# One branch a step for the second products of a mixture-of-experts layer, and later requests for the rows of the norms

## The chip, the cores and the metric

The kernel runs on one core of one Trainium2 chip. The metric is the device time of one execution in microseconds (us); smaller is better. Times of runs are medians of several executions; a profile is one execution more, taken with the hardware profiler on.

## What is computed

Three layers in a row, all in fp32, over 2304 tokens of width 512. The matrix products split each fp32 number into a high and a low part and take three products (high by high, high by low, low by high).

```python
x = windowed_attention(q, k, v)                 # window 64, 4 x 576 tokens, 8 heads
xn = x / sqrt(mean(x * x) + 1e-6) * rms_g       # first MoE, dense, d_ff 1536
x = (silu(xn @ w_gate) * (xn @ w_val)) @ w_out
e = argmax(x @ wg2); p = softmax(x @ wg2)[e]    # second MoE, 8 experts, d_ff 1024
out = p * (relu(x @ w1[e]) @ w2[e])             # each token through its own expert
```

## The kernel before

The order of every engine's instructions is the order in which the program is written out (a manual schedule); nothing is reordered later. TensorE (PE) is fed by one helper, `mm` at L57, so all matrix products have that line. LDWEIGHTS, branches and other instructions of PE's sequencer stand in the profile as PEld and PEldq.

**The first MoE.** The 2304 tokens are six sub-blocks of 384 (`subs`), in four blocks of two, two, one and one (`BLOCKS`). The loop over `units` (L900 on) goes block by block through 12 slices of d_ff, and one unit is one slice for one sub-block: 24 products of 384 columns (gate and value), SiLU on ScalarE (ACT, L649), a product on VectorE (DVE, L650), a split into `hh` and `hl` (L651, L652), and then the nine output products of the unit before. Beside that, generators hand out further work piece by piece: `beside` (L274) resumes each task while the unit has budget; a task that yields "step" gets a rest of 99, so it is not resumed again in this unit.

- `conversion` / `w_conv` (L391): the weights of the first block come as 64-bit words, half a slice (768 KB) at a time into three buffers `st`, by a DMA that SyncE (SP) issues at L389, and are turned into fp32 by ACT (L472, L464, L465) and DVE (L429, L434, L438). The ACT part of the next half stands on ACT ahead of the next unit's SiLU.
- `norms` / `norm(i)` (L308, L312): the norms of sub-blocks 2 to 5, one after the other. Each asks for its rows (L323, on SP, into the one buffer `xr`), yields, squares them on ACT (L332), sums, takes a root by Newton steps, and writes the split `xt` (L368, L371). The last thing that reads `xr` is the DVE subtraction at L371. The next norm's request is written out in the same piece that ends the norm before, and SP waits at it until `xr` is free.
- L923: in every second unit from 2 to 16, SP issues a fill of 1 MB for one expert (`xs<-x2dram`).

SP's queue is in order: an instruction that waits holds all that are behind it.

**The second MoE.** `route` has sorted the tokens by expert into `xs` and `table`. `items` (L809) are the pieces of work: two of two tiles for expert 0 (a tile is 128 tokens), then one "full" item of up to four tiles for each of experts 1 to 7. Each item has 8 steps `(i, f)`, one for each 128 of d_ff, 72 in all (`steps2`). Step k (L1100 on) does the first products of k (`first_mm`, 12 of n columns, into bank k % 2), the second products of step k - 1 (`out_c`, three for each tile j, summed over f into bank 4 + j), then `relu(k)` on ACT and DVE (L1020, L1021), the split of the weights for step k + 2 (`c_split`, L552 and L554) and loads of weights (L822). Transposes of the next item's tokens stand behind steps 2 to 5 (`c_transpose`, L856). At f = 0 `c_out` scales and writes out the item before (L1050 on ACT for tiles 0 and 2, L1048 on DVE for 1 and 3, L1051 on POOL), which empties banks 4 to 7.

How many of an item's tokens are real is known only at run time. `count[e]` is loaded into a register of PE, and `cases(i, body, unit)` (L984) writes the body out once for each possible size and branches to the right one by halving: for a full item in units of 64 the sizes 512, 448, 384, 320, 256, with three comparisons on the way to 256, which is the last in the code; in units of 128 the sizes 512, 384, 256. A body has its `first_mm` at that size (never under 256 columns) and its `out_c` for as many tiles. With three matrix products to a tile, a full item's step with f > 1 is written out as 5 x 12 first products and 12 + 12 + 9 + 9 + 6 second ones: 108 pairs of LDWEIGHTS and MATMUL, of which 18 to 24 run. The order of bodies in the code is 512, 448, 384, 320, 256.

Step f = 1 has two sets of branches, one around the first and one around the second products; step f = 0 has one around the first products and one around the second products of the item before. `last_tiles` (L1030) finishes the last item.

Of the kernel before, what the change touches and what calls it, by code (L numbers as in the profile page):

```python
# [26 lines left out]
P = 128  # L27
# [23 lines left out]
def attention_moe_moe_kernel(ctx, tc, qT, kT, vw, w1p, rms_g, wg2, wg2T, w2p, out):  # L51
# [4 lines left out]
    def mm(o, l, r, start, stop):  # L56
        nc.tensor.matmul(o, l, r, start=start, stop=stop)  # L57
# [54 lines left out]
    def xt_views(at, n):  # L112

        return [xt_t[:, a:a + 4 * n].rearrange("p (c t) -> p c t", c=4) for a in (at, at + 4 * n)]

    def big(which):
        return xr_p.tile([P, 4, 512], F32, name="xr" if which == 0 else "sq")
# [156 lines left out]
    def beside(tasks, budget):  # L274

        for t in tasks:
            t.rest = 0.0
        while budget > 0:
            can = [t for t in tasks if not t.done and t.rest <= 0 and t.want != "bank"
                   and not (callable(t.want) and not t.want())]  # L280
            if not can:
                break
            cost = can[0].piece()
            budget -= cost
            for o in tasks:
                if o is not can[0]:
                    o.rest -= cost
        return budget

    def on_bank(tasks, bk):  # L290

        for t in tasks:
            if t.want == "bank" and not t.done:
                return t.piece(bk)
        return 0.0
# [16 lines left out]
    def norm(i):  # L312
        t0, nt, _ = subs[i]
        if i == 1:

            xr, sq = (t[:, :4 * SUB].rearrange("p (c t) -> p c t", c=4) for t in wraw_t[:-3:-1])
        else:
            xr, sq = big(0), big(1)
        done = 0
        while done < nt:  # L320
            b, s = divmod(t0 + done, S)
            step = min(nt - done, S - s)
            nc.sync.dma_start(xr[:, :, done:done + step],  # L323
                              xdram[b][:, :, s:s + step].rearrange("h p t -> p h t"))
            done += step
        for _ in range(4 if i < 2 else 1):
            yield "step"
        for c in range(4):
            if i < 2:
                nc.gpsimd.tensor_tensor(out=sq[:, c, :nt], in0=xr[:, c, :nt], in1=xr[:, c, :nt], op=ALU.mult)  # L330
            else:
                nc.scalar.activation(sq[:, c, :nt], xr[:, c, :nt], AF.Square, scale=1.0)  # L332
            if i < 2 and c % 2:
                yield "step"
        yield "step"
        for a, b in ((0, 1), (2, 3), (0, 2)):
            (nc.gpsimd if i < 2 else nc.vector).tensor_add(sq[:, a, :nt], sq[:, a, :nt], sq[:, b, :nt])
            if i == 0:
                yield "step"
            elif i > 1:  # L340
                yield 0.5
        if i == 1:
            yield "step"
        bk = yield "bank"
        mm(bk[:, :nt], ones, sq[:, 0, :nt], True, True)
        m, y, t = (sq[:, k, :nt] for k in (1, 2, 3))
        nc.vector.tensor_scalar(out=m, in0=bk[:, :nt], scalar1=1.0 / DM, scalar2=1e-6, op0=ALU.mult, op1=ALU.add)
        yield 0.5
        nc.vector.tensor_scalar(out=y.bitcast(I32), in0=m.bitcast(I32), scalar1=-0.5, scalar2=1597463007.0,
                                op0=ALU.mult, op1=ALU.add)  # L350
        yield 0.4
        sc = 1.0
        for _ in range(NEWTON):

            nc.scalar.activation(t, y, AF.Square, scale=1.0 / sc)
            yield "rest"
            nc.vector.tensor_mul(t, t, m)
            yield 0.6
            nc.vector.scalar_tensor_tensor(out=y, in0=t, scalar=-3.0, in1=y, op0=ALU.add, op1=ALU.mult)
            yield 0.6  # L360
            sc = sc * -2.0
        yield lambda: i < NXT or free[0] >= i - NXT + 1
        xh_t[i], xl_t[i] = xh, xl = xt_views(i % NXT * 8 * SUB, nt)
        for c in range(5):
            if c < 4:
                nc.vector.scalar_tensor_tensor(out=xr[:, c, :nt], in0=xr[:, c, :nt], scalar=gs_sb[:, c:c + 1],
                                               in1=y, op0=ALU.mult, op1=ALU.mult)
                nc.scalar.copy(xh[:, c], xr[:, c, :nt])  # L368
                yield 0.5
            if c > 0:  # L370
                (nc.gpsimd if i == 0 else nc.vector).tensor_tensor(  # L371
                    out=xl[:, c - 1], in0=xr[:, c - 1, :nt], in1=xh[:, c - 1].bitcast(F32), op=ALU.subtract)
                yield 0.0 if i == 0 else 0.5
        normed[0] = i
# [153 lines left out]
    def split_mm(o, lh, ll, rh, rl, start, stop):  # L528
        mm(o, lh, rh, start, False)
        mm(o, lh, rl, False, False)  # L530
        mm(o, ll, rh, False, stop)
# [123 lines left out]
    def last_mm(w, h, banks, f0, f1):  # L655

        wh, wl, hh, hl = wh_t[w, "o"], wl_t[w, "o"], hh_t[h], hl_t[h]
        for j, bk in banks:
            ts = slice(j * P, (j + 1) * P)
            split_mm(bk, hh[:, ts], hl[:, ts], wh, wl, f0, f1)  # L660
# [9 lines left out]
    def out_b(u):  # L670
        k, i = units[u]
        last_mm(k, ("b", u), enumerate(out_banks(i)), u == starts[i], u == stops[i])
# [147 lines left out]
    def c_load(w):  # L820
        if w < E * NF2:
            nc.sync.dma_start(wring[w % NRING], w2p[w // NF2, w % NF2])  # L822
# [77 lines left out]
    for u, (k, i) in enumerate(units):  # L900
        n = steps[k][0]
# [82 lines left out]
    def cases(i, body, unit=P // 2):  # L984

        e, t0, T = items[i]

        def between(lo, hi):
            if lo == hi:
                return body(lo * unit)  # L990
            mid = (lo + hi) // 2
            with tc.If(count[e] > t0 * P + mid * unit) as more:
                between(mid + 1, hi)
            with more.Else():
                between(lo, mid)

        if i == 0:
            body(T * P)
        elif T == 4:
            between(2 * P // unit, T * P // unit)  # L1000
        else:
            unit = P
            between(1, T)

    def first_mm(k, n):
        i, f = steps2[k]
        wh, wl = wh_t[K0 + k, "a"], wl_t[K0 + k, "a"]
        xh, xl, n = xh_t["c", i], xl_t["c", i], max(n, 2 * P)
        for c in range(4):
            w = slice(c * P, (c + 1) * P)  # L1010
            split_mm(bank[k % 2][:, :n], wh[:, w], wl[:, w], xh[:, c, :n], xl[:, c, :n], c == 0, c == 3)
# [12 lines left out]
    def out_c(k, n, j0=0):  # L1024
        f = steps2[k][1]
        last_mm(K0 + k, K0 + k, [(j, bank[4 + j]) for j in range(j0, -(-n // P))], f == 0, f == NF2 - 1)

    NL = len(steps2) - 1
# [71 lines left out]
    for k, (i, f) in enumerate(steps2):  # L1100
        if i == 0:
            first_mm(k, 2 * P)
            if k == 0:
                out_b(len(units) - 1)
            else:
                on_bank([end], bank[3])
                beside([end], 99)
                out_c(k - 1, 2 * P)
        elif f == 1:

            cases(i, lambda n: first_mm(k, n))
            cases(i, lambda n: out_c(k - 1, n), P)
        elif f > 0:
            j0 = 2 if k >= NL - 1 else 0
            cases(i, lambda n: (first_mm(k, n), out_c(k - 1, n, j0)))
        else:
            parts = [lambda: cases(i, lambda n: first_mm(k, n)), lambda: cases(i - 1, lambda n: out_c(k - 1, n), P)]
            for part in parts[::-1] if i == 1 else parts:
                part()
        relu(k)  # L1120
        if k == 0:
            evac(len(units) - 1)
        if f == 0 and i > 0:
            c_split(k + 2, parts="a")
            c_out(i - 1)
            c_split(k + 2, parts="o")
        else:
            c_split(k + 2)
        while i > 0 and later:
            c_load(later.pop(0))  # L1130
        if i == 0:
            if f == NF2 - 1:
                end.finish(bank[3])
                load_count(1)
                for j in range(2):
                    c_transpose(1, j, bank[2 + j % 2])
            continue
        if f == 5:
            load_count(i + 1)
        beside([over], 0.4)  # L1140
        if i == len(items) - 1 and f == 3:

            nc.gpsimd.drain()
        if f in (2, 3, 4, 5):
            c_transpose(i + 1, f - 2, bank[2 + f % 2])
        if f == 6:
            c_gather(i + 2)
# [85 lines left out]
```

## Time and profile before

| | us |
|---|---|
| median of 3 runs | 870.89 (869.74 to 874.89) |
| the profiled execution | 877.16 |
| span of the profiled execution, first to last instruction | 875.3 |
| PE busy with matrix products in it | 842.8 |
| mean granted clock of PE, share of full | 0.989 |

The span is cut by the profile into the attention (to about 130 us), the first MoE (to about 594 us) and the second (to about 870 us). The profiled execution is longer than the median of the runs by 6.27 us. In the views, a time in square brackets is how long the engine sat idle before an instruction and what ended that; "issue" means that nothing which the profile shows ended it. Idle time of an engine matters only where PE waits for it.

### The profile page before, as it was taken

What the parts mean: (1) busy time and instruction counts of PE and PEld (TensorE: products, weight loads), DVE (VectorE), ACT (ScalarE), POOL (GpSimd) and SP (SyncE); (2) the same over time, 40 slices, a digit from 0 to 9 for tenths busy, and PEclk for the clock granted to TensorE, in tenths of its full rate; (3) what the DMA queues carried; (4) which work ended last, traced back from release to release, by engine and by line L of the source; (5) the groups of instructions that cost most, each with busy time, mean ns of one, the idle gap of its engine ahead of it and who ended that gap; (6) DMA issues with size and microseconds to landing.
All of it is one profiled execution on the core that took longest, in us unless ns stands there. A gap on an engine that the chain in (4) does not pass through costs nothing. (4 is left out here: it accounts for less than half of the span.)

```text
span 875.3 us, 13523 instructions
## 1 busy us (share of the span) xinstructions
PE 842.8 (96%) x4667; PEld 775.9 (89%) x4667; DVE 607.8 (69%) x1472; ACT 450.0 (51%) x993; POOL 212.2 (24%) x227
## 2 busy tenths in 40 slices
PE   7999999999899999999999999999999999988997
PEld 7999988999799999999989999988888898867886
DVE  6789878788685566666478864697685765655454
ACT  5787787777573433322243424334564645554353
POOL 3348573444242000000500032004300120121011
PEclk9999999999899999999999999999999999999999
DMA  7988618895922300000220016533674655552000
GB/s 215 303 267 265 201 69 228 194 227 121 248 103 97 108 19 19 1 0 1 73 73 1 1 37 176 199 107 133 213 258 151 208 204 172 182 198 82 12 35 29
DMA packets 47071, 114.49 MB, mean 131 GB/s; under 512 B 10223, under 2 KB 14703, under 8 KB 46834
## 3 DMA queue, kind: packets, MB, share of 16 engines
q1 hardware_dynamic: 42386, 103.50, 38.6%
q0 software_dynamic: 4576, 9.47, 2.9%
q8 instruction: 77, 1.26, 0.6%
q14 instruction: 32, 0.26, 0.1%
HBM read 93.90 MB, written 31.10 MB: 143 GB/s over the span
## 5 line engine op out<-in xcount | busy, mean ns | idle before, releaser
L57 PE MATMUL bank<-xt,wha 128*128 128x384 f32 (+3 forms) x1728 | 422.6, 329 | 14.6 <-issue 9.6
L57 PEld LDWEIGHTS bank<-xt,wha 128*128 128x128 f32 x1728 | 306.1, 190 | 31.1 <-issue 11.0
L57 PE MATMUL bank<-xt,wla 128*128 128x384 f32 (+3 forms) x864 | 281.9, 326 | 0.7 <-DVE wla L554 0.7
L57 PEld LDWEIGHTS bank<-xt,wla 128*128 128x128 f32 x864 | 164.2, 190 | 2.2 <-DVE wla L554 1.7
L57 PE MATMUL bank<-who,hl 128*128 128x512 f32 x382 | 151.6, 397 | 0.6 <-DVE hl L1021 0.6
L57 PE MATMUL bank<-wlo,hh 128*128 128x512 f32 x382 | 151.8, 397 | 0.0
L57 PE MATMUL bank<-who,hh 128*128 128x512 f32 x382 | 151.2, 396 | 0.5 <-ACT hh L651 0.2
L651 ACT CAST hh<-t 128x384 fp32r<-128x384 f32 x72 | 37.0, 513 | 144.5 <-DVE t L650 142.2
L554 DVE TENSOR_TENSOR wla<-wraw,wha 128x512 fp32r<-128x512 f32 (+1 forms) x112 | 97.8, 874 | 8.1 <-ACT wha L552 7.4
L1021 DVE SCALAR_TENSOR_TENSOR hl<-bank,hh 128x512 fp32r<-128x512 f32 (+1 forms) x71 | 44.6, 628 | 80.8 <-ACT hh L1020 79.7
L650 DVE TENSOR_TENSOR t<-t,bank 128x384 f32<-128x384 f32 x72 | 39.8, 552 | 85.1 <-PE bank L57 61.9
L552 ACT CAST wha<-wraw 128x512 fp32r<-128x512 f32 (+1 forms) x113 | 87.1, 771 | 7.6 <-DVE wraw L438 7.0
L1020 ACT ACTIVATE hh<-bank 128x512 fp32r<-128x512 f32 (+1 forms) x71 | 39.1, 550 | 97.8 <-PE bank L57 96.8
L57 PEld LDWEIGHTS bank<-who,hl 128*128 128x128 f32 x382 | 72.4, 190 | 17.6 <-DVE hl L1021 1.4
L1051 POOL DMA_INDIRECT out_dram<-x,ix x32 | 34.9, 1091 | 218.2 <-ACT x L1050 211.2
L57 PEld LDWEIGHTS bank<-who,hh 128*128 128x128 f32 x382 | 72.8, 191 | 12.1 <-issue 0.6
L57 PEld LDWEIGHTS bank<-wlo,hh 128*128 128x128 f32 x382 | 72.7, 190 | 11.1
L57 PE MATMUL bank<-kt,qz 128*128 128x128 f32 x288 | 76.3, 406 | 5.3 <-DMA kt<-in_kT_dram 4.5
L552 ACT CAST who<-wraw 128x512 fp32r<-128x512 f32 x111 | 68.7, 619 | 22.5 <-PE bank L57 20.7
L57 PEld LDWEIGHTS bank<-kt,qz 128*128 128x128 f32 x288 | 72.4, 334 | 5.8 <-issue 4.5
L554 DVE TENSOR_TENSOR wlo<-wraw,who 128x512 fp32r<-128x512 f32 x99 | 68.0, 687 | 13.1 <-ACT who L552 6.0
L715 DVE SCALAR_TENSOR_TENSOR junk<-x,wg_bc 128x512 f32<-128x512 f32 x120 | 75.9, 686 | 0.0
(168 smaller groups left out, 977.3 us busy)
## 6 DMA issues: line engine op xcount, KB each, us to landing
wraw<-in_w2p_dram SPq DMA_DIRECT2D x64, 512.0 KB
st<-in_w1p_dram SPq DMA_DIRECT2D x24, 768.0 KB
wraw<-in_vw_dram SPq DMA_DIRECT2D x16, 512.0 KB
xs<-x2dram SPq DMA_DIRECT2D x8, 1024.0 KB
qz<-in_qT_dram SPq DMA_DIRECT2D x32, 144.0 KB
xdram<-wraw SPq DMA_DIRECT2D x16, 288.0 KB
x2dram<-x SPq DMA_DIRECT2D x18, 256.0 KB
kt<-in_kT_dram SPq DMA_DIRECT2D x15, 288.0 KB
```

The lines of the kernel that those rows point to most:

```text
L57: nc.tensor.matmul(o, l, r, start=start, stop=stop)
L552: nc.scalar.copy(wh, src[:, r])
L554: e.tensor_tensor(out=wl, in0=src[:, r], in1=wh.bitcast(F32), op=ALU.subtract)))
L650: nc.vector.tensor_tensor(out=t, in0=t, in1=v, op=ALU.mult)
L651: nc.scalar.copy(hh[:, :nt], t)
L715: nc.vector.scalar_tensor_tensor(out=junk, in0=x2, scalar=1.0, in1=wg_bc[:, e], op0=ALU.mult, op1=ALU.mult, accum_out=lg[:, j, e:e + 1])
L1020: nc.scalar.activation(hh[:, :n], bank[k % 2][:, :n], AF.Relu, scale=1.0)
L1021: nc.vector.scalar_tensor_tensor(out=hl[:, :n], in0=bank[k % 2][:, :n], scalar=0.0, in1=hh[:, :n].bitcast(F32), op0=ALU.max, op1=ALU.subtract)
L1051: d = nc.gpsimd.indirect_dma_start(out=out[:, :], in_=y, in_offset=None, out_offset=bass.IndirectOffsetOnAxis(ap=ix[:, j, 0:1], axis=0), b ...
```

## The change

Two edits. In `norm`, for sub-blocks 3, 4 and 5, a "step" is yielded before the rows are asked for, so that the request is written out one unit later. In the loop over `steps2`, the branches are cut differently:

- full items, f > 0: one set of branches around `first_mm(k)` and the second products of tiles 2 and 3; the second products of tiles 0 and 1 follow behind the branches, without any. So f = 1 has one set where it had two. For k of 70 and 71 the step is as before.
- full items, f = 0: branches around the first products as before, then tiles 0 and 1 of the item before without a branch, then branches around its tiles 2 and 3 only. For the item behind the two-tile items, as before.
- the second two-tile item (i = 1): no branches around the first products of f = 0 and 1, which always have 256 columns.

```diff
@@ norm @@
         else:
+            if i > 2:
+                yield "step"
             xr, sq = big(0), big(1)
@@ the loop over steps2 @@
-        elif f == 1:
-
+        elif i == 1:
+            if f < 2:
+                if f == 0:
+                    out_c(k - 1, 2 * P)
+                first_mm(k, 2 * P)
+                if f == 1:
+                    cases(i, lambda n: out_c(k - 1, n))
+            else:
+                cases(i, lambda n: (first_mm(k, n), out_c(k - 1, n)))
+        elif f > 0:
+            cases(i, lambda n: (first_mm(k, n), out_c(k - 1, n, 2)))
+            if k < NL - 1:
+                out_c(k - 1, 2 * P)
+        else:
+            j0 = 0 if i == 2 else 2
             cases(i, lambda n: first_mm(k, n))
-            cases(i, lambda n: out_c(k - 1, n), P)
-        elif f > 0:
-            j0 = 2 if k >= NL - 1 else 0
-            cases(i, lambda n: (first_mm(k, n), out_c(k - 1, n, j0)))
-        else:
-            parts = [lambda: cases(i, lambda n: first_mm(k, n)), lambda: cases(i - 1, lambda n: out_c(k - 1, n), P)]
-            for part in parts[::-1] if i == 1 else parts:
-                part()
+            out_c(k - 1, j0 * P)
+            cases(i - 1, lambda n: out_c(k - 1, n, j0), P)
```

Written out, a full item's step with f > 1 becomes 5 x 12 first products, 6 + 6 + 3 + 3 + 0 second ones in the bodies and 6 behind them: 84 pairs. A whole full item goes from 822 pairs (87 + 87 + 6 x 108) to 663 (75 + 7 x 84). The products that run are the same ones.

## Rows read from the trace of the kernel before

**Rows 1.** The page's first lines: span and busy time of each engine.
```profile
span 875.3 us, 13523 instructions
...
PE 842.8 (96%) x4667; PEld 775.9 (89%) x4667; DVE 607.8 (69%) x1472; ACT 450.0 (51%) x993; POOL 212.2 (24%) x227
```
**Rows 2.** PE's timeline in the first MoE: its longest idle time there.
```profile
225.93 1.65 PE L57 MATMUL bank<-sq,ones 128*128 128x384 f32 x2 [4.09 <-DVE t L650]
```
**Rows 3.** ACT's timeline there: when the next half of the weights is used.
```profile
209.43 0.91 ACT L472 ACTIVATE wraw<-st 128x768 f32<-128x768 f32 x1
...
222.36 0.89 ACT L472 ACTIVATE wraw<-st 128x768 f32<-128x768 f32 x1 [5.44 <-DMA st<-in_w1p_dram]
```
**Rows 4.** SP's timeline there: start us, us, what is issued.
```profile
198.22 0.33 SPq L389 DMA_DIRECT2D st<-in_w1p_dram  x1
208.54 0.38 SPq L323 DMA_DIRECT2D xr<-xdram  x1
208.96 0.51 SPq L923 DMA_DIRECT2D xs<-x2dram  x1
209.58 1.24 SPq L389 DMA_DIRECT2D st<-in_w1p_dram  x2
```
**Rows 5.** SP's waits, whole run: us in total, times, longest us.
```profile
SPq L323 <- DVE xt L371: 57.8, 3, 32.1
```
**Rows 6.** A window: length, busy of PE, PEld, DVE, ACT, POOL, clock, DMA share, GB/s.
```profile
202.60:208.80 6.20, 6.20 (x34) 5.83 (x33) 6.02 (x8) 4.39 (x7) 3.69 (x2) 1.00 0.00 0
```
**Rows 7.** The same view of two stretches at the lower clock.
```profile
746.90:750.30 3.40, 3.40 (x14) 2.92 (x13) 1.29 (x2) 1.10 (x2) 0.00 (x0) 0.50 0.75 288
...
224.70:231.50 6.80, 5.58 (x15) 4.97 (x16) 3.77 (x6) 4.39 (x7) 1.01 (x1) 0.50 0.96 178
```
**Rows 8.** PE's first products by shape, 644 to 869.7 us: busy, mean ns | idle before.
```profile
L57 PE MATMUL bank<-xt,wha 128*128 128x256 f32 x256 | 50.2, 294 | 10.8 <-issue 9.6 <-ACT xt L858 1.2
...
L57 PE MATMUL bank<-xt,wha 128*128 128x320 f32 x64 | 14.6, 315 | 0.7 <-ACT who L552 0.3 <-ACT wha L552 0.3
```
**Rows 9.** PE's timeline in the second MoE: the longest idle times.
```profile
690.11 0.50 PE L57 MATMUL bank<-xt,wha 128*128 128x256 f32 x2 [1.17 <-ACT xt L858]
...
746.05 0.50 PE L57 MATMUL bank<-xt,wha 128*128 128x256 f32 x2 [1.91 <-issue]
...
774.62 0.50 PE L57 MATMUL bank<-xt,wha 128*128 128x256 f32 x2 [2.28 <-issue]
780.10 0.50 PE L57 MATMUL bank<-xt,wha 128*128 128x256 f32 x2 [1.95 <-issue]
797.50 0.50 PE L57 MATMUL bank<-xt,wha 128*128 128x256 f32 x2 [3.02 <-issue]
```
**Rows 10.** The branches of `cases` (L992): all, then one (ns min/median/max, first and last).
```profile
L992 PEldq COMPARE_BRANCH  x218: 65/208/5391, 621.0 to 863.5; - x109
...
L992 PEldq COMPARE_BRANCH  x1: 3221/3221/3221, 771.3 to 771.3; - x1
```
**Rows 11.** PE's timeline: two steps of a 256-column item that follow each other.
```profile
763.72 0.40 PE L57 MATMUL bank<-xt,wha 128*128 128x256 f32 x2
...
766.54 0.40 PE L57 MATMUL bank<-xt,wha 128*128 128x256 f32 x2
```
**Rows 12.** The page's DMA queues: packets, MB, share of 16 engines.
```profile
q8 instruction: 77, 1.26, 0.6%
```
**Rows 13.** `last_tiles`, where a body is empty: L992, and PE around it.
```profile
L992 PEldq EVENT_SEMAPHORE  x1: 51/51/51, 865.9 to 865.9; - x1
...
865.44 0.39 PE L57 MATMUL bank<-who,hl 128*128 128x512 f32 x1
865.98 0.47 PE L57 MATMUL bank<-who,hh 128*128 128x512 f32 x1
```
**Rows 14.** Emptying banks 4 and 6 (ACT), then the next second products (PE).
```profile
706.51 1.27 ACT L1050 ACTIVATE x<-bank,ix 128x512 f32<-128x512 f32 x2
...
708.79 0.39 PE L57 MATMUL bank<-who,hh 128*128 128x512 f32 x1
```

## The prediction

> **What bounds it.** I read the page first: PE is busy for 842.8 of 875.3 us [rows 1], so a gain can only come from time in which PE stands still or runs at the lower clock. PE's timeline gives those places, and I followed each to its cause.
>
> In the first MoE there is one large place. [...] The cause stands on ACT: L472 waits 5.44 us for its half of the weights [rows 3], and the SiLU behind it comes late. Why those weights are late is seen on SP: between 198.55 and 208.54 it issues nothing, because it waits at the norm's request L323 for DVE's L371, and the fill and the weight load stand behind it [rows 4, 5]. Meanwhile the DMA engines move nothing at all: share 0.00, 0 GB/s from 202.60 to 208.80 [rows 6].
>
> In the second MoE, PE's idle time by shape says where to look: 10.8 us stand before the first products of 256 columns, 0.7 before those of 320, nothing before 384 and 448 [rows 8]. The 256 products are four full items (256 rows are 4 x 64), the short ones. The five longest gaps are 1.17, 1.91, 2.28, 1.95 and 3.02 us [rows 9]; the rest of the 10.8 is one of about 0.5. Most are marked "issue", so no engine ended them. The branches tell: a branch takes 208 ns in the median and 5391 at most, and the one just before the gap of 2.28 us takes 3221 [rows 10]. The instruction behind it was not there yet: instructions come by DMA, 77 packets of 1.26 MB together, 16.4 KB each [rows 12]. Behind three of the gaps the clock is at half for 3.40 us with PE busy throughout; one of the three stands in [rows 7]. That is 3 x 1.7 = 5.1 us. Gaps and clock together: 10.8 + 0.7 + 5.1 = 16.6 us. These are what the branches cost now.
>
> **The norm's request.** Norm 3's load moves past the fill and one weight load on SP. Their order becomes: weight load (198.22), fill at once, next weight load as soon as its buffer is free, then the request, which still can't go before 208.54. So the rows come no sooner and no later on SP, but behind two transfers, 1 MB and 0.77 MB, that now use the idle stretch. From 198.6, at the 178 and 288 GB/s of the stretches in [rows 7], 1.8 MB take 6 to 10 us, so the weights land by 209. They are wanted one unit after 209.43, at about 215.7: 6 us to spare. ACT's wait of 5.44 us goes, and with it the idle time and the half clock behind it: -6.9 us. What is late next is the norm itself: squares and Newton steps come one unit later, with two dozen units before their result is used, so this costs 0; were that cover gone, it would be one unit's squares on ACT, under 2 us. Bounds: 0 if the next weight load is late instead, -6.9 if nothing is. I take -6.9, since 6.2 us of idle DMA time are there to be used. The requests of norms 4 and 5 account for most of SP's 57.8 us of waiting [rows 5], but hold only stores that PE does not wait for: 0.
>
> **The branches in short items.** A full step's written code falls from 108 pairs to 84, what runs stays. One such step takes 766.54 - 763.72 = 2.82 us [rows 11]. For the same length of code PE now passes through 108 / 84 as much work, 3.63 us instead of 2.82: each wait for code is met by 0.8 us more work. Taking 0.8 from each gap leaves 0.4, 1.1, 1.5, 1.15 and 2.2. The two of 1.91 and 2.28 stand right behind step f = 1, where a second set of branches with 27 written pairs and 6 that run makes the distance between two waits short; that set goes, so I take these two as gone. What stays is 0.4 + 1.15 + 2.2 = 3.7 us, and behind the longest one stretch of low clock, 1.7: 5.4 us. The gain is 16.6 - 5.4 = 11.2 us. Bounds: 16.6 if all goes; 3.2 if the gaps fall only as the written code of an item does (822 to 663, 19%); below nothing in the third rival.
>
> **The empty body.** At f = 0 the branch around tiles 2 and 3 of the item before has an empty body if that item was short. Such a body is seen once, in `last_tiles`: instead of products there is a semaphore instruction of 51 ns that lets PE run dry, and the next product starts 0.54 us after the one before, where 0.23 is usual: 0.31 lost [rows 13]. Three full items come behind a short one. In each, the three branches of f = 1 then find PE with no work queued: 3 x 0.208. So 0.31 + 0.62 = 0.93, three times: +2.8 us. Bounds: 0.9 if the branches are hidden, 10.6 if each also meets a wait of 3.22 as in [rows 10]. I take 2.8, as code was there for most branches (median 208 ns).
>
> [...]
>
> **At no cost.** In items with more than two tiles, tile 2 now comes ahead of tile 0, so at f = 1 bank 6 is wanted first. ACT has emptied it at 706.51 + 1.27 = 707.78, and the second products start at 708.79 [rows 14]: 1.0 us to spare; without that cover it would cost at most that one move, 0.6 us, in three items. The branches dropped from the two-tile item were hidden (no gap there by the branches): 0, at best a few tenths.
>
> **Sum.** -6.9 - 11.2 + 2.8 = -15.3 us against the profiled execution's 877.16: 861.9. The median of the runs is 6.27 us lower. If these runs have every stall that the profile shows, they go to 870.89 - 15.3 = 855.6; if the 6.27 us are stalls that they do not have, they end where the profile ends, at 861.9. Waits for code vary from one execution to the next, and the runs themselves lie 5.1 us apart, so I take the middle: 859.
>
> **Rivals**, each on the same middle (3.1 us under the profile's own sum).
>
> 1. The gaps stay. A wait arises when the path enters new code, not by how far it jumps, and falls only with the amount of code: -6.9 - 3.2 + 2.8 = -7.3, 866.7. For it: two branches waited 4 to 5.4 us, more than any step's work, and nothing makes a load itself faster. Against: the gaps stand only in short items, where much code is passed per us of work.
> [...]
> 2. All gaps go and the empty bodies cost the least: -6.9 - 16.6 + 0.9 = -22.6, 851.4. For it: nothing waits in items of 384 and 448. Against: 5391 ns is more than a step.
> 3. Slower: every shortened body ends as the empty one does. If the sizes under 512 must make up for missing tiles with a semaphore instruction that runs PE dry, 7 items x 7 steps lose 0.31 each, 15.2 us, and the lead that hides waits for code is lost too, so those gaps stay: -6.9 + 15.2 + 2.8 = +11.1, 885. It turns the result from 0.08 us a step on, if the gaps stay. Against it: bodies with fewer tiles exist before, and among 218 branches the trace has one such instruction [rows 10, 13].
> 4. The first MoE's stall comes back with the next weight load, because fill, rows and weights want the DMA engines together: -11.2 + 2.8, 865.6. Against: the idle 6.2 us.
>
> **Chances.** Forecast 0.48, rivals 0.18, 0.22, 0.05, 0.07. The range, 849.5 to 867.5, holds the forecast's bounds and rivals 1, 2 and 4. A change of 1% (8.7 us, below 862.2) is about what the measurement can tell. Faster by more than that: most of the forecast and rival 2, and a quarter of rivals 1 and 4, 0.67; within 1%: 0.28; slower: 0.05.
>
> **What would show it.** Right: no wait of ACT for `st` in the first MoE, SP's fill at about 198.6, no low clock between 200 and 240 us; in the second MoE gaps before the 256 products of about 4 us instead of 10.8, few branches over 3000 ns, and fewer than 77 instruction packets; three semaphore instructions at L992 more, each with about 1 us of idle PE. Wrong: gaps as large as before behind other steps, semaphore instructions in every step, or a stall at the next weight load.

## The result, and the profile after

The changed kernel takes 859.45 us in the median of six runs (858.1 to 864.49), the kernel before 872.0 in six runs on the same chip (869.74 to 874.89): ratio 0.9864, 95% interval 0.9834 to 0.9894. In a second comparison it was 858.58 against 873.23, ratio 0.9831 (0.981 to 0.9852). So it is faster by 1.4 to 1.7%, some 12.5 to 14.7 us. The forecast was 859.0, in a range of 849.5 to 867.5.

The page's first lines, of after:

```profile
span 857.1 us, 13511 instructions
...
PE 834.9 (97%) x4667; PEld 770.3 (90%) x4667; DVE 606.8 (71%) x1472; ACT 449.3 (52%) x993; POOL 210.6 (25%) x227
...
q8 instruction: 68, 1.11, 0.6%
```

The span is shorter by 18.2 us than that in [rows 1]. The same 4667 products take 7.9 us less busy time, since none before the last instructions runs at the lower clock any more (mean granted clock 1.00, 0.989 before), and the idle time fell by 10.3 (875.3 - 842.8 = 32.5 against 857.1 - 834.9 = 22.2). There are 68 packets of instructions where [rows 12] has 77.

**The first MoE.** SP's timeline of after (L391 is the weight load, L925 the fill, L325 the norm's request), and ACT's next use of the weights:

```profile
198.58 0.48 SPq L925 DMA_DIRECT2D xs<-x2dram  x1
204.16 0.33 SPq L391 DMA_DIRECT2D st<-in_w1p_dram  x1
208.53 0.38 SPq L325 DMA_DIRECT2D xr<-xdram  x1
210.45 0.33 SPq L391 DMA_DIRECT2D st<-in_w1p_dram  x1
```
```profile
209.42 0.91 ACT L474 ACTIVATE wraw<-st 128x768 f32<-128x768 f32 x1
215.90 0.92 ACT L474 ACTIVATE wraw<-st 128x768 f32<-128x768 f32 x1
218.40 1.75 ACT L334 ACTIVATE sq<-xr 128x384 f32<-128x384 f32 x4
221.56 0.91 ACT L474 ACTIVATE wraw<-st 128x768 f32<-128x768 f32 x1
```

Against [rows 4] the fill goes out 10.4 us sooner and the weight load 5.4 sooner, while the norm's request stays at 208.5, because its buffer is free no earlier. ACT finds its weights at 215.90 without waiting; in [rows 3] it waited until 222.36. What the DMA engines and PE do there, the same windows as before:

```profile
202.60:208.80 6.20, 6.20 (x34) 5.81 (x33) 6.02 (x8) 4.40 (x7) 3.69 (x2) 1.00 0.99 107
208.80:215.30 6.50, 6.50 (x36) 6.10 (x35) 5.32 (x7) 4.75 (x7) 1.72 (x1) 1.00 1.03 349
...
222.00:232.00 10.00, 10.00 (x56) 9.59 (x55) 8.42 (x10) 7.43 (x11) 5.14 (x3) 1.00 0.82 228
```

The 6.2 us in which nothing was moved [rows 6] have a DMA share of 0.99, and PE is busy throughout at clock 1.00, where [rows 2, 7] had 4.09 us of idle time and half the clock.

**The second MoE.** PE's products by shape from 637 to 851.5 us, idle time behind the bar; compare [rows 8]:

```profile
L57 PE MATMUL bank<-xt,wha 128*128 128x256 f32 x256 | 48.6, 287 | 2.5 <-ACT x L1052 1.2 <-ACT who L554 0.5 <-issue 0.4
L57 PE MATMUL bank<-xt,wla 128*128 128x256 f32 x128 | 36.3, 283 | 1.5 <-issue 1.5
L57 PE MATMUL bank<-xt,wha 128*128 128x448 f32 x64 | 18.6, 372 | 0.6 <-ACT x L1052 0.6
L57 PE MATMUL bank<-xt,wha 128*128 128x384 f32 x64 | 16.8, 342 | 0.6 <-ACT x L1052 0.6
L57 PE MATMUL bank<-xt,wha 128*128 128x320 f32 x64 | 14.6, 315 | 0.2 <-issue 0.2
```

Of 11.5 us of idle time, 5.4 are left. PE's timeline names most of it:

```profile
676.99 0.38 PE L57 MATMUL bank<-xt,wla 128*128 128x256 f32 x1 [1.51 <-issue]
...
699.24 0.61 PE L57 MATMUL bank<-xt,wha 128*128 128x384 f32 x2 [0.58 <-ACT x L1052]
...
759.49 0.50 PE L57 MATMUL bank<-xt,wha 128*128 128x256 f32 x2 [1.20 <-ACT x L1052]
...
769.63 0.50 PE L57 MATMUL bank<-xt,wha 128*128 128x256 f32 x2 [0.53 <-ACT who L554]
779.66 0.51 PE L57 MATMUL bank<-xt,wha 128*128 128x256 f32 x2 [0.44 <-issue]
787.14 0.67 PE L57 MATMUL bank<-xt,wha 128*128 128x448 f32 x2 [0.59 <-ACT x L1052]
```

And the branches, now L994:

```profile
L994 PEldq COMPARE_BRANCH  x200: 70/208/2857, 617.6 to 845.6; - x100
L994 PEldq EVENT_SEMAPHORE  x4: 51/51/51, 698.7 to 847.7; - x4
```

Four semaphore instructions stand where [rows 13] has one. The three new ones belong to the idle times 0.58, 1.20 and 0.59, each in front of step f = 1 of a full item behind a short one: 2.37 us that the change brought with it. What remains of waits for code is 1.51 + 0.53 + 0.44 + 0.15 = 2.6 us, with no low clock behind it (the longest branch now takes 2857 ns, 5391 in [rows 10]). The names in the brackets of the gaps (ACT L1052, L554) are only the last update before the product: L1052 empties the banks of the item before and `who` is a weight of the second products, and a first product reads neither.

### The profile page after: what moved, and what is told of

Read it like the earlier page. It is cut to its first block, busy times and chain, and to the rows that moved or that the text cites. A ratio compares the mean times of both kernels' runs of the same rounds, so it can differ in the third digit from the quotient of the medians.

```text
span 857.1 us, 13511 instructions
## 1 busy us (share of the span) xinstructions
PE 834.9 (97%) x4667; PEld 770.3 (90%) x4667; DVE 606.8 (71%) x1472; ACT 449.3 (52%) x993; POOL 210.6 (25%) x227
## 5 line engine op out<-in xcount | busy, mean ns | idle before, releaser
L554 ACT CAST wha<-wraw 128x512 fp32r<-128x512 f32 (+1 forms) x113 | 87.1, 771 | 8.1 <-DVE wraw L440 7.7
L57 PEld LDWEIGHTS bank<-who,hh 128*128 128x128 f32 x382 | 71.9, 188 | 11.9 <-issue 0.6
L554 ACT CAST who<-wraw 128x512 fp32r<-128x512 f32 x111 | 68.7, 619 | 17.5 <-PE bank L57 16.1
```

Source lines behind the costliest of these rows:

```text
L554: nc.scalar.copy(wh, src[:, r])
```

## The experiments

Two comparisons, each against the kernel before on one chip.

**The changed kernel again.** 

> The changed kernel once more, for comparison with the others of this call on the same chip. Both theories: ratio to the kernel before 0.985 to 0.988, about 859.5 us.

858.58 us, ratio 0.9831 (0.981 to 0.9852), a little lower than expected. Its profile has the same three idle times in front of f = 1 (0.58, 1.19, 0.67), and not the one of 1.51: waits for code differ from one execution to the next.

**The norm's edit alone.**

```diff
         else:
+            if i > 2:
+                yield "step"
             xr, sq = big(0), big(1)
```

> The kernel before with the norm's edit alone. Theory (SP's wait at the request held the weight load, in every execution): ACT's wait of 5.44 us for the weights and PE's idle 4.09 us go, the half clock from 224.7 to 231.5 goes, -6.9 us, ratio about 0.992, and the second half of the run has its gaps as before (12 to 17 us of idle time and half clock in the profile). Rival (the stall is of the profiled execution only, or moves to the next weight load): within 2 us of the kernel before, ratio 0.998 or more.

867.26 us, ratio 0.9937 (0.9915 to 0.996): -6.0 us. The low clock and the idle time of the first MoE are gone, and SP's order there is that of after, to 0.1 us. In the second MoE the idle time stands as before, 11.9 us before the 256 products where [rows 8] has 10.8, with two stretches of low clock instead of three (the views by shape of the experiments cover 636 to 880 us, so their counts differ a little):

```profile
L57 PE MATMUL bank<-xt,wha 128*128 128x256 f32 x257 | 50.2, 293 | 11.9 <-issue 9.2 <-ACT xt L860 2.7
```

The rival's ratio of 0.998 lies outside the interval, so the stall isn't one of the profiled execution alone, and the theory holds.

**Norm 3 alone.**

```diff
+            if i == 3:
+                yield "step"
```

> The kernel before with the norm's edit for sub-block 3 alone; norms 4 and 5 ask as before. Theory: the whole gain of the norm's edit (6.0 us alone) is that of norm 3, ratio 0.992 to 0.995, and SP still waits some 48 us in two waits at L323. Rival: part of it comes from norms 4 and 5, ratio over 0.996.

866.73 us, ratio 0.9929 (0.9908 to 0.9951), -6.1: the whole gain is that of norm 3. SP's remaining waits:

```profile
SPq L325 <- DVE xt L373: 51.8, 3, 32.1
```

In [rows 5] they were 57.8 us. The expectation had two waits of 48 us together, and there are three: norm 3's own request still waits some 4 us until 208.58, 6 us less than before. The waits of norms 4 and 5 are still there and cost nothing that the runs show (-6.1 here, -6.0 with all three moved).

**The branches' edit alone** (the second part of the change's diff).

> The kernel before with the second MoE's edit alone. Theory: the stall of 4.09 us in the first MoE stands as before; the gaps in the second MoE fall to about 5 us with the empty bodies' in it, no low clock there; against the median of the runs this is what is left of the 12.5 us after the norm's 6.9: -5 to -6 us, ratio 0.993 to 0.994. Rival (the gaps of the second MoE are mostly of the profiled execution): -2 us or less, ratio 0.998 or more.

864.94 us, ratio 0.9913 (0.9893 to 0.9933): -8.3 us, more than expected. The idle time of the first MoE stands there, in its old size (the low clock behind it lasts 3.4 us in this profile, 6.8 in that of before):

```profile
226.16 1.65 PE L57 MATMUL bank<-sq,ones 128*128 128x384 f32 x2 [4.28 <-DVE t L650]
```

-6.0 and -8.3 add up to -14.3, and both together gave -14.65 in the same comparison: within the intervals the two edits add up. On the profile's scale this edit gave 877.16 - 865.45 = -11.7 us.

**No empty body.**

```diff
-            j0 = 0 if i == 2 else 2
+            j0 = 0 if i == 2 else 1
             cases(i, lambda n: first_mm(k, n))
             out_c(k - 1, j0 * P)
             cases(i - 1, lambda n: out_c(k - 1, n, j0), P)
```

> The changed kernel, but at f = 0 of the full items from the fourth item on, tile 0 alone stands ahead of the branches and tiles 1 to 3 stand inside, so that no body is empty. Theory (the empty body lets PE run dry and bares the three branches that follow; the profile of after has 0.58 + 1.20 + 0.59 = 2.37 us there): the three semaphore instructions at the line of the branches go, these three gaps go, and the time falls by 2.4 us against the changed kernel, to about 857, ratio to before about 0.983. Rival (PE would stand still there anyway, because the branches of f = 1 follow at once on those of f = 0): the gaps stay at 0.4 us or more each and the time falls by under 1 us.

856.28 us (854.73 to 857.34), ratio 0.9816 (0.9796 to 0.9837), 2.3 us under the changed kernel in the same comparison. The runs of the two overlap a little (the changed kernel's go down to 856.9), but the profile shows where the time went: the three semaphore instructions are gone, and with them the idle time before the products of 384 and 448 columns and most of that before 256.

```profile
L994 PEldq EVENT_SEMAPHORE  x1: 51/51/51, 843.4 to 843.4; - x1
...
L57 PE MATMUL bank<-xt,wha 128*128 128x256 f32 x264 | 49.8, 286 | 0.8 <-ACT xt L860 0.8
...
L57 PE MATMUL bank<-xt,wha 128*128 128x448 f32 x64 | 18.5, 370 | 0.0
L57 PE MATMUL bank<-xt,wha 128*128 128x384 f32 x64 | 16.7, 341 | 0.0
```

The rival falls. This is the fastest version that ran.

**More code that never runs.**

```diff
+        elif T == 4 and unit < P:
+            between(2 * P // unit, T * P // unit + 2)
         elif T == 4:
             between(2 * P // unit, T * P // unit)
...
-                return body(lo * unit)
+                return body(min(lo * unit, T * P))
```

> The changed kernel with two more bodies (a size of 640 and one of 576, both at 512 columns) written ahead of the 512 one in the branches in units of 64 of the full items. No count reaches them, so the same products run, and the way to the 256 body has three comparisons as before. A full item is written out in 939 pairs (changed kernel 663, kernel before 822). Theory A (waits come with the amount of code that is passed per us of work): the gaps before the 256 products come back to the kernel before's or beyond, +8 to +15 us against the changed kernel, 867 to 873 us, ratio to before 0.993 to 1.000, and about 83 instruction packets on q8 for 68. Theory B (it is the number of sets of branches, and that work stands behind them): as the changed kernel, 857 to 860, ratio 0.982 to 0.986, with more packets but no more gaps.

886.69 us, ratio 1.0153 (1.0118 to 1.0188): some 28 us slower than the changed kernel, nearly twice what theory A expected at most (the profile has 20 us more idle time of PE than that of after). With code that no count reaches, and with the same cut of the branches as the changed kernel, the gaps are larger than before:

```profile
L57 PE MATMUL bank<-xt,wha 128*128 128x256 f32 x258 | 51.2, 296 | 20.3 <-issue 14.9 <-ACT xt L860 3.1 <-DVE xt L1025 1.7
...
L57 PE MATMUL bank<-xt,wha 128*128 128x320 f32 x64 | 15.3, 328 | 3.1 <-issue 2.0 <-ACT wha L554 1.1
...
L994 PEldq COMPARE_BRANCH  x216: 65/208/5568, 617.7 to 874.7; - x108
...
779.66 0.80 PE L57 MATMUL bank<-xt,wha 128*128 128x256 f32 x2 [4.26 <-issue]
```

The instruction packets are 84, about as expected. Theory B falls. (The padding also lengthens the jumps and gives the items of 384 and 448 columns a third comparison; this run doesn't separate them from the amount of code.)

**One set of branches at f = 1, nothing else.**

```diff
-        elif f == 1:
+        elif f == 1 and i == 1:
 
             cases(i, lambda n: first_mm(k, n))
             cases(i, lambda n: out_c(k - 1, n), P)
```

> The kernel before with one edit: in the full items step f = 1 has one set of branches around first and second products, as f > 1 has. An item is written out in 843 pairs instead of 822. Theory A (amount of code): as the kernel before or a little slower, ratio 0.998 to 1.003. Theory B (number of sets): the gaps behind f = 1 (1.91 and 2.28 us in the profile of before) go with the half clock behind them, -4 to -7 us, ratio 0.992 to 0.995. The prediction took part of B: it let these two gaps go with the second set.

876.59 us, ratio 1.0033 (1.0002 to 1.0064): a little slower. The gaps behind f = 1 are gone, but as large ones now stand one step earlier, in front of f = 1. L1050, which empties the banks of the item before at the end of f = 0, shows the place: here it comes just before the gap, in the kernel before a whole step of products lies between (740.69 and 769.18, gaps at 746.05 and 774.62 [rows 9]).

```profile
744.26 1.37 ACT L1050 ACTIVATE x<-bank,ix 128x512 f32<-128x512 f32 x2 [0.28 <-PE bank L57]
746.94 0.51 PE L57 MATMUL bank<-xt,wha 128*128 128x256 f32 x2 [2.04 <-ACT who L552]
...
771.19 1.27 ACT L1050 ACTIVATE x<-bank,ix 128x512 f32<-128x512 f32 x2
774.40 0.50 PE L57 MATMUL bank<-xt,wha 128*128 128x256 f32 x2 [2.87 <-issue]
```

They were 1.91 and 2.28 us and are 2.04 and 2.87. Dropping the second set doesn't remove these waits, it moves them, and there are 21 pairs more in an item; theory B's gain of 4 to 7 us doesn't come.

**Tiles 0 and 1 behind the branches for f > 1, nothing else.**

```diff
-            cases(i, lambda n: (first_mm(k, n), out_c(k - 1, n, j0)))
+            if i == 1 or k >= NL - 1:
+                cases(i, lambda n: (first_mm(k, n), out_c(k - 1, n, j0)))
+            else:
+                cases(i, lambda n: (first_mm(k, n), out_c(k - 1, n, 2)))
+                out_c(k - 1, 2 * P)
```

> The kernel before with one edit: in the steps f > 1 of the full items tiles 0 and 1 stand behind the branches; f = 0 and f = 1 as before, with two sets each. An item is written out in 678 pairs, nearly as few as in the changed kernel, and no body is empty at f = 0. Theory A (amount of code): nearly all of the branches' part of the gain (8.3 us for it alone), plus the 2.3 us of the empty bodies: -8 to -11 us, ratio 0.987 to 0.991. Theory B (number of sets): the gaps behind f = 1 stay, -3 to -5 us, ratio 0.994 to 0.997.

866.45 us, ratio 0.9932 (0.9905 to 0.9958): -6.4 us, between the two expectations. This is the bulk of the branches' gain, with both sets at f = 0 and 1 kept. And in its profile no idle time over 0.25 us stands behind f = 1 of the two items that had 1.91 and 2.28 there; what is left in the second of them stands in front of f = 3 and f = 7:

```profile
772.70 0.50 PE L57 MATMUL bank<-xt,wha 128*128 128x256 f32 x2 [0.62 <-issue]
786.59 0.50 PE L57 MATMUL bank<-xt,wha 128*128 128x256 f32 x2 [1.03 <-ACT who L552]
```

So those gaps go with less code, the second set still in place. The version has no empty bodies, but gives less than expected from that; the 1.9 us to the branches' edit alone lie within the intervals, so whether the second set costs something of its own stays open.

Five versions of the second MoE, ordered by the pairs that an item is written out in:

| pairs in an item | version | packets on q8 | norm's edit | against before, us |
|---|---|---|---|---|
| 663 | branches alone | 68 | no | -8.3 |
| 678 | f > 1 alone | 69 | no | -6.4 |
| 822 | before | 77 | no | 0 |
| 843 | one set at f = 1 | 78 | no | +3.8 |
| 939 | padded | 84 | yes | +13.9, so about +20 without the norm's 6.0 |

The time follows the amount of code, and more steeply the more there is. The packets follow it too, so what is written out is loaded, whether it runs or not.

That the idle times are waits for these packets is seen in the traces, which hold the time of each packet. In the ten profiles PE stands idle 30 times for 1 us or more in front of a first product of a full item (the three waits at 1.2 us behind an empty body not counted), and each time it goes on 1.4 to 2.1 us after a packet of q8 has ended. Before the gap that ends at 746.05 in the kernel before the packet is this one (DMA view of 743.2 to 744.4 us: packets, MB, share of 16 engines):

```profile
q8 instruction: 1, 0.02, 5.5%
```

No two of these packets start less than 3.0 us apart in any profile (3.00 at the least in that of before, 3.07 in that of after). An estimate from that: 16 packets more for 7 x 276 pairs are 121 pairs a packet, so an item of 663, 822 or 939 pairs needs 16, 20 or 23 us for its code alone, and a short item's products take about 8 x 2.82 = 23 us [rows 11]. The padded version is at that limit.

## Why the prediction was right

- **The norm's request**, -6.9: right in place, cause and size (-6.0 alone, 0.9 less). The 6.9 is the 4.09 us of idle time [rows 2] and half of the 5.58 us in which PE was busy at clock 0.50 [rows 7]. No run shows that half by itself; half of it and of the 3 x 3.40 us at 0.50 in the second MoE would be 7.9 us, and PE's busy time fell by 7.9 from before to after. The steps are in the profile: the fill at 198.58 (forecast 198.6), the request unmoved at 208.5, no wait at 215.90 (forecast: wanted at about 215.7), squares one unit later at no cost. One step was too quick: the weights were to land by 209 at 178 to 288 GB/s, but the window of the fill moved 107 GB/s, and the last packet of the load issued at 204.16 ended at about 213.3. Some 2.6 us were to spare, not 6. Rival 4, that the stall comes back with the next load, did not happen: ACT uses the next half at 221.56 without a wait.
- **The gaps of the short items**, -11.2: right in sum on the runs' scale, since it and the empty bodies make -8.4, and the edit alone gave -8.3. On the profile's scale, from which the term was worked out, the edit gave -11.7, so part of this closeness is luck. Three steps inside were not as argued. The residue was forecast at 5.4 us with one stretch of low clock; the profile of after has 2.6 and none. Taking 0.8 us from each gap was too little: the one of 3.02, in front of f = 7, is 0.44 at the same place in after. And I let the gaps behind f = 1 go because the second set of branches goes: one set at f = 1 alone, in 843 pairs, only moves them one step, and with 678 pairs they go with the second set still there. They went because the whole step carries less code. The argument of more work per length of code was the right one, and it alone gave most of the gain.
- **The empty body**, +2.8: 2.37 us in the profile, 2.3 us in the runs of the version without it. Three places, each with its semaphore instruction, as forecast; singly they are 0.6, 1.2 and 0.6 instead of 0.93 each. The branches themselves take 208 ns in the median, before [rows 10] and after.
- **At no cost**: the order of tiles 2 and 3 ahead of 0 and 1. The second products, which would wait for bank 6 or 7, have 0.1 us of idle time in front of them in after, so the banks were free in time:

```profile
L57 PE MATMUL bank<-who,hh 128*128 128x512 f32 x143 | 56.2, 393 | 0.1
```

- **The level.** The profile of before (877.16) is above 25 of the 26 runs of that kernel in the three comparisons (869.63 to 877.91). Taking the middle between "all stalls are in the runs" and "the 6.27 us aren't" gave 859.0, against 859.45 and 858.58. The profile itself fell by 18.2 us, more than the 15.3 of the sum; the runs fell by 12.5 to 14.7. So the closeness to 859.0 owes something to the middle; the sum of the terms alone is good to about 3 us on either scale.
- **The rivals.** Rival 1 had the mechanism (waits come with the amount of code) but let them fall only in proportion, 19%; the runs show a fall by far more (the edit alone gave -8.3 with the empty bodies' 2.3 in it, rival 1 had -3.2), and the padded version a rise by far more. Long jumps alone don't explain the waits: on the way to the 256 body of before the longest jump passes two bodies of 24 pairs, 0.4 of a packet by the estimate of 121 pairs a packet, and branches waited up to 5391 ns [rows 10]; after, PE stands still for 1.51 us where there is no jump at all, and goes on 1.4 us after a packet of q8 has ended. So code that is merely next in order was late too. Rival 3 did not occur: four semaphore instructions, not one in every step.

## What to carry to other kernels

Code that is written out for cases costs time even if it never runs (some 28 us for 276 pairs more in each item here): where PE's work per step is short (2.82 us in the short items), keep out of the branches all that every case does, and count the instructions that a step passes, not those that it runs. A branch body that can be empty may become a wait that lets the engine run dry (0.58 to 1.20 us of idle time each); leave one piece of work in it. And in an in-order queue, put a request whose buffer is not yet free behind the transfers that could already go: SP's queue issued nothing for 10.0 us behind one [rows 4], and the move gave 6.0 us.

## What the runs showed that was not expected

- A wait for code needs no branch: at 676.99 PE stands still for 1.51 us in the middle of twelve products written in a row, after the eighth, with nothing that ended it. The profile of the branches' edit alone has one of 0.85 us at the same place (684.36).
- The effect is steep: 276 pairs more in an item than the changed kernel's 663, none of them run, cost some 28 us, with single gaps up to 4.26 us.
- In the changed kernel's second profile the granted clock falls from full to half for 3.4 us near 600 us, where PE has no idle time (0.72 in the mean of the 6 us below). Just before, from 595.48 on, it does 24 products of only 8 columns. Those products, and the window view (length, PE busy and count, PEld, DVE, ACT, POOL, clock, DMA share, GB/s):

```profile
595.48 2.74 PE L57 MATMUL bank<-wg_sb,x 128*128 128x8 f32 x24
...
598.00:604.00 6.00, 6.00 (x30) 5.31 (x31) 4.72 (x26) 2.51 (x6) 0.60 (x3) 0.72 0.01 3
```

Five of the ten profiles have this stretch, and the products of 8 columns are in all. What makes the clock fall there in some and not in others stays open.
